# Sliding-window attention on one Trainium2 core: 16 heads to a step, the Exps issued right behind their logits, and a reordered start

## The chip, the cores and the metric

The kernel runs on one core of a Trainium2 chip. The metric is device time in microseconds (us below); the span that the profile gives, from the first to the last instruction, is about 2 us shorter. Executions of the kernel before lie between 1249 and 1257 us; each trace shows one execution.

Engine names as the profile has them: PE is TensorE (matmul), PEld its weight loads, DVE VectorE, ACT ScalarE, POOL GpSimd, SP SyncE, which here only issues DMAs. In this kernel matmuls write to PSUM and read their operands from SBUF, two on-chip memories; a DMA is a transfer that runs beside the engines.

## The reference, cut to what matters

```python
x = A_x                                        # 2048 x 576
x = x + A(layernorm(x)); x = x + B(layernorm(x))
x = x + A(layernorm(x)); x = x + B(layernorm(x))

def A(x):                                      # 32 heads of 18
    q, k, v = split(x @ wqkv)
    # each position attends to 8 positions: itself and 2, 4, ... 14 before it
    attn = softmax(q . k * scale over those 8)
    return (attn . v) @ wo

def B(x):                                      # gated MLP with a 2048 x 2048 mix over positions
    z1, z2 = split(gelu(x @ w_in))
    return (z1 * (w_sp @ layernorm(z2) + b_sp)) @ w_out
```

Below, layers 1 and 3 are the attention layers A, layers 2 and 4 the mixers B. The mixers take three quarters of the time and are not touched.

## The kernel before

A tile of 112 queries (19 tiles) takes a dense block of logits per head against 128 keys; a mask is built into the padded rows of Q and K, so that Exp alone makes the window. A head has 18 of 32 rows, so four heads lie in the four 32-row groups of the PE array. The loop works on a quarter tile `u` of 8 heads, and spreads other matmuls, the "fill work", over the loop from a table: the rest of the Q/K projections (`PG`), values (`VW`), output projections (`WO`).

```python
def H_tile(self, name):                    # logits: 2 buffers of 2 PSUM banks
    return self.ps.tile([P, 2, 512], f32, name=name, tag="H", bufs=2)
# O_tile: tag "O", 2 banks, probabilities x values.  PT_tile(any_bank=False): tag "PT", 2 banks, fill work

def L_mm(u):                               # logits of 8 heads: 2 row groups x 4 groups of heads
    t, hf, jp = half(u)
    L_tiles[u] = L_ps = self.H_tile("L_ps")
    for ftl in range(4):
        for jj in range(2):
            j = 2 * jp + jj                # row group 0,1 (jp 0) or 2,3 (jp 1)
            nc.tensor.matmul(L_ps[:nk, jj, ...], lhsT=kT[32*j:32*j+32, ...], rhs=qT[32*j:32*j+32, ...],
                             tile_position=(32 * j, 0), ...)
def EXP(u):                                # one ACTIVATE of 128 x 896, PSUM -> SBUF
    nc.scalar.activation(out=P_bufs[u % 4]..., in_=Lv..., func=ACT.Exp, scale=scale)
def PV(u): ...                             # 8 matmuls, 19 columns each, into O_ps
def NORM(u): ...                           # after every second u: DVE reciprocal and multiply into o_t;
                                           # after a whole tile SP transposes o_t into the ring oT by DMA
def PG(d, qk, cc, dve, queues): ...        # 5 matmuls, PSUM copy by DVE or ACT into stg, 7 stores into QK
def VW(t, hh, dve): ...                    # 5 matmuls, PSUM copy into v_ext
def WO(i, hh): ...                         # 5 matmuls on oT and wo_sb, add and layernorm on DVE and POOL

# ... cut: the start of layer 1 (loads, masks, layernorm, first projections) ...
for d, qk, cc in pgs[:4]:
    PG(d, qk, cc, False, q2)
for k_, (d, qk, cc) in enumerate(pgs[4:]):
    at((k_ * 30) // 16, PG, d, qk, cc, k_ % 2 == 0)
for i in range(NS):
    u = 4 * t + (12 if t < NT - 3 else 10) # t: the last tile that rows of block i need
    at(u, WO, i, 0); at(u + 1, WO, i, 1)   # ... and its loads, layernorm, stores
if li == 0:
    at(1, self.load_wo, nc.gpsimd)
L_mm(0)
for u in range(NU):                        # NU = 76
    EXP(u)
    if u + 1 < NU:
        L_mm(u + 1)
    for f, a in table.pop(u, []):          # fill work of this quarter
        f(*a)
    if u >= 1:
        PV(u - 1)
        if u % 2 == 0:
            NORM(u - 1)
```

In the traces here ACT works off its instructions in the order of the program (an example is at 656.21 us below). So Exp u+1 stands behind the PSUM copies of the fill work of quarter u, which wait for PE.

The softmax here doesn't subtract the row's maximum and nothing guards it: scores larger than these inputs give would overflow.

## Time and profile before

| | before |
|---|---|
| median | 1253.6 us (4 runs, 1250.1 to 1256.5) |
| span of the profiled execution (a fifth run, 1253.2 us) | 1250.7 us |
| start to the first logits of layer 1 | 52.7 us |
| loop of layer 1, first logits to last output projection | 118.2 us |
| layer 2 | 464.8 us |
| layer 3, projections ahead of the loop | 31.4 us |
| loop of layer 3 | 114.4 us |
| layer 4 | 469.2 us |

From the page, the share of the span that PE is busy, and the clock granted to it in 40 equal slices (9 is 90% or more):

```profile
PE 1204.0 (96%) x8428; PEld 647.5 (52%) x8528; DVE 542.2 (43%) x1202; ACT 388.4 (31%) x609; POOL 277.6 (22%) x371
...
PEclk9899999999999999999999999999999999999999
```

PE looks full. The same by stretches, one row each for the start, the loop of layer 1 (from its first in-loop projection at 57.0 us, behind the wait of 4.0 us below, to the mixer), layer 2, the loop of layer 3 (to the mixer) and layer 4. PEclk is the granted clock, as a share of full speed; the DMA share is the busy share of the 16 DMA engines as the profile reckons it, and can exceed 1:

```profile
core 0: us, PE busy (x) PEld busy (x) DVE busy (x) ACT busy (x) POOL busy (x), PEclk, DMA share, GB/s
0.00:52.70 52.70, 35.80 (x171) 17.91 (x176) 36.19 (x110) 22.18 (x35) 20.44 (x60) 0.97 0.62 155
57.00:163.70 106.70, 100.31 (x1564) 73.98 (x1572) 63.12 (x178) 70.71 (x98) 57.70 (x68) 0.98 0.74 159
171.00:635.70 464.70, 462.38 (x2438) 230.24 (x2474) 188.24 (x373) 106.14 (x179) 66.21 (x87) 1.00 0.25 64
667.00:775.60 108.60, 102.00 (x1602) 75.95 (x1609) 64.04 (x180) 75.14 (x104) 56.30 (x66) 1.00 0.80 169
781.50:1250.70 469.20, 462.80 (x2439) 229.93 (x2474) 168.98 (x310) 93.15 (x164) 55.48 (x57) 1.00 0.20 49
```

The mixers have no gaps worth naming: of the 6.4 us of layer 4 in which PE isn't busy the waits view names 1.3, and this trace lacks some matmul records (2439 in layer 4). In the loops PE is idle for 6 to 7 us each, at the start for 17. Whom PE waited for, longest in total first (us, times, longest):

```profile
PE L_ps L405 <- ACT P_sb L413: 11.6, 31, 0.8
...
PE pp L380 <- DMA xnT<-ln_xn: 4.0, 1, 4.0
...
PE pp L380 <- ACT stg L352: 2.9, 2, 2.0
```

The first line is the one that the change aims at: logits wait 31 times, in both layers together 11.6 us, for an Exp that frees their PSUM tile. The next two lines are the start. One more, left out here: output projections wait once, 1.3 us, for an `oT` transpose.

But a group that counts as busy can still be slow. From the timeline of PE in layer 3 (start us, length us, then the matmuls merged; what follows starts when the array lets it):

```profile
667.09 0.40 PE L405 MATMUL L_ps<-QK 32*128 32x112 bf16 x16
667.42 0.79 PE L358 MATMUL pv<-wv_sb,xnT 128*128 128x288 bf16 x5
...
672.07 0.35 PE L424 MATMUL O_ps<-v_ext,P_sb 128*128 128x19 bf16 x8
672.35 0.37 PE L405 MATMUL L_ps<-QK 32*128 32x112 bf16 x8
672.65 0.36 PE L424 MATMUL O_ps<-v_ext,P_sb 128*128 128x19 bf16 x8
673.72 0.37 PE L405 MATMUL L_ps<-QK 32*128 32x112 bf16 x8 [0.71 <-ACT P_sb L413]
```

Read it by starts, not by lengths: 8 logits matmuls hold PE from 672.35 to 672.65, 0.30 us. 16 in a row, which happens only where the loop begins, hold it from 667.09 to 667.42, 0.33 us. In the single records of the trace the 8 go in pairs 49 ns apart and leave a tail of 0.14 us; the 16 go in pairs about 25 ns apart. The last line is one of the waits.

### The profile page before, as it was taken

How to read it: one execution, taken by the hardware profiler on the slowest of the kernel's cores; microseconds unless marked ns; L12 is line 12 of the kernel's file. 1: busy time of each engine (PE TensorE's matmuls, PEld its weight loads, DVE VectorE, ACT ScalarE, POOL GpSimd, SP SyncE). 2: the span in 40 equal slices, each digit the busy share in tenths (PEclk: the TensorE clock that was granted, in tenths of full speed). 3: DMA queues.
4: the chain of work that ended last, by engine and by line, in shares of the span. 5: the costliest groups of instructions: out<-in, count | busy, mean ns of one | idle time of the engine just before them, and what ended most of it. 6: DMA issues, size and time to landing. Idle time of an engine off the chain costs nothing.

```text
span 1250.7 us, 20588 instructions
## 1 busy us (share of the span) xinstructions
PE 1204.0 (96%) x8428; PEld 647.5 (52%) x8528; DVE 542.2 (43%) x1202; ACT 388.4 (31%) x609; POOL 277.6 (22%) x371
## 2 busy tenths in 40 slices
PE   5799999999999999999998999999999999999998
PEld 3367754444444444447755677444444444444577
DVE  9246658633223323324552567674322332232321
ACT  4366757701110111011146676774011011101000
POOL 2346567400000000001132466772000000000000
PEclk9899999999999999999999999999999999999999
DMA  5678779000000000046644797960000000000342
GB/s 163 119 166 175 155 163 231 4 18 12 11 11 1 11 11 11 1 152 172 174 105 113 169 198 171 193 134 22 1 11 12 11 11 11 11 1 1 125 118 72
DMA packets 175686, 101.56 MB, mean 81 GB/s; under 512 B 134296, under 2 KB 155864, under 8 KB 175592
## 3 DMA queue, kind: packets, MB, share of 16 engines
q1 hardware_dynamic: 163632, 76.70, 27.6%
q0 software_dynamic: 6448, 17.67, 5.4%
q10 hardware_dynamic: 5512, 5.88, 1.5%
q8 instruction: 66, 1.08, 0.3%
q14 instruction: 28, 0.23, 0.1%
HBM read 42.39 MB, written 16.53 MB: 47 GB/s over the span
## 4 chain that ended last, share of the span: by engine, by line
PE 86%; POOL 3%; ACT 3%; issue 3%; DVE 2%; DMA 1%; SPq 1%; POOLq 0%; ACTq 0%; DVEq 0%
PE pg L794 40%; PE pz L776 12%; PE po L848 11%; PE pz L699 10%; PE pp L380 6%; PE pv L358 3%; ACT P_sb L413 2%; POOL ln_xn L235 2%; PE L_ps L405 2%; PE pw L453 2%; PE pzs L699 1%; PE O_ps L424 1%; DVE QK L182 1%; DVE ln_st L497 1%; ACT stg L352 1%
## 5 line engine op out<-in xcount | busy, mean ns | idle before, releaser
L794 PE MATMUL pg<-Wq,Z 128*128 128x512 bf16 x2256 | 500.0, 379 | 2.4
L794 PEld LDWEIGHTS <-Z 128*128 128x128 bf16 x2304 | 225.5, 98 | 271.8
L798 DVE TENSOR_TENSOR g_tmp<-pg,ln_xn 128x512 f32<-128x512 f32 x144 | 99.6, 692 | 429.1 <-PE pg L794 417.2
L788 ACT ACTIVATE z1T<-pz 128x1024 bf16<-128x1024 f32 x72 | 73.7, 1023 | 513.9 <-PE pz L776 513.7
L848 PE MATMUL po<-wout,Z 128*128 128x288 bf16 x1152 | 141.4, 286 | 0.0
L77 POOL DMA_DIRECT2D wout<-in_B_w_out_dram x4 | 4.3, 1064 | 604.6 <-PE pg L794 604.6
L776 PE MATMUL pz<-xnT,w 128*128 128x512 bf16 (+1 forms) x630 | 135.0, 380 | 1.1 <-issue 0.6
L413 ACT ACTIVATE P_sb<-L_ps 128x896 bf16<-128x896 f32 (+1 forms) x152 | 127.5, 893 | 12.1 <-PE L_ps L405 11.8
L848 PEld LDWEIGHTS <-Z 128*128 128x128 bf16 x1152 | 112.7, 98 | 28.8
L699 PEld LDWEIGHTS <-xnT 128*128 128x128 bf16 (+1 forms) x800 | 66.5, 97 | 82.6 <-issue 24.9
L380 PE MATMUL pp<-xnT,wqk_sb 128*128 128x512 bf16 x378 | 96.0, 394 | 10.4 <-DMA xnT<-ln_xn 4.0
L799 DVE TENSOR_TENSOR Z<-g_tmp,z1T 128x512 bf16<-128x512 f32 x144 | 99.7, 692 | 9.7
L699 PE MATMUL pz<-win2a,xnT 128*128 128x512 bf16 x366 | 101.2, 380 | 1.2 <-ACT zp L713 0.8
L776 PEld LDWEIGHTS <-w 128*128 128x128 bf16 (+1 forms) x640 | 51.1, 97 | 80.0 <-issue 27.1
L713 ACT ACTIVATE zp<-pz 128x1024 bf16<-128x1024 f32 x64 | 65.5, 1023 | 45.7 <-PE pz L699 30.2
L235 POOL TENSOR_SCALAR ln_xn<-x_new,ln_mv,ln_rstd 128x576 bf16<-128x576 f32 x32 | 75.5, 2361 | 3.3
L380 PEld LDWEIGHTS <-wqk_sb 128*128 128x128 bf16 x400 | 38.8, 101 | 54.2 <-issue 16.0
L858 DVE TENSOR_TENSOR x_new<-po,xo 128x288 f32<-128x288 f32 (+1 forms) x64 | 28.8, 456 | 87.8 <-PE po L848 87.8
L699 PE MATMUL pz<-win2b,xnT 128*128 128x512 bf16 (+1 forms) x256 | 65.9, 380 | 0.7
L405 PE MATMUL L_ps<-QK 32*128 32x112 bf16 (+1 forms) x1216 | 54.9, 208 | 11.9 <-ACT P_sb L413 11.6
L358 PE MATMUL pv<-wv_sb,xnT 128*128 128x288 bf16 (+1 forms) x380 | 60.6, 294 | 0.2 <-ACT xnT L516 0.2
L715 DVE CUSTOM_DVE_ANT_0 Z<-zp 128x1536 bf16<-128x1536 bf16 x32 | 56.2, 1756 | 7.8 <-ACT zp L713 7.8
(102 smaller groups left out, 932.0 us busy)
## 6 DMA issues: line engine op xcount, KB each, us to landing
xres<-x_new SPq DMA_DIRECT2D x48, 288.0 KB
xo<-xres SPq DMA_DIRECT2D x48, 288.0 KB
wout<-in_B_w_out_dram POOLq DMA_DIRECT2D x4, 1296.0 KB, 10.0
QK<-stg SPq DMA_DIRECT2D x64, 72.0 KB
QK<-stg POOLq DMA_DIRECT2D x64, 72.0 KB, 3.7
w<-in_B_w_in_dram SPq DMA_DIRECT2D x16, 256.0 KB
win2a<-in_B_w_in_dram POOLq DMA_DIRECT2D x12, 288.0 KB, 5.0
wqk_sb<-in_A_wqkv_dram ACTq DMA_DIRECT2D x2, 1152.0 KB
```

The costliest lines, as they stand in the source:

```text
L235: e.tensor_scalar(out=xn[:nrows, 0:D], in0=x_t[:nrows, :], scalar1=mv[:nrows, 0:1], scalar2=rstd[:nrows, 0:1], op0=ALU.subtract, op1=ALU.mult)
L358: nc.tensor.matmul(pv[:nk, 0:288], lhsT=self.xnT[:, c, QT * t:QT * t + nk], rhs=wv_sb[:, c, hh * 288:(hh + 1) * 288], start=(c == 0), stop ...
L380: nc.tensor.matmul(pp[:, :], lhsT=w, rhs=self.xnT[:, c, PADL + cc * 512:PADL + (cc + 1) * 512], start=(c == 0), stop=(c == 4))
L405: nc.tensor.matmul(L_ps[:nk, jj, ftl * QT:ftl * QT + nq], lhsT=kT[32 * j:32 * j + 32, g, QT * t:QT * t + nk], rhs=qT[32 * j:32 * j + 32, g ...
L413: nc.scalar.activation(out=P_bufs[u % 4][:nk, :, :, 0:nq], in_=Lv[:nk, :, :, 0:nq], func=ACT.Exp, scale=scale)
L699: nc.tensor.matmul(pzvs[ci][:, sub * 512:sub * 512 + w], lhsT=self.xnT[r0:r1, c, PADL + i * P:PADL + (i + 1) * P], rhs=win2(c)[r0:r1, c0 + ...
L776: nc.tensor.matmul(pz1s[q // 2][:, q % 2, :], lhsT=w1[r0:r1, c, sub * P:(sub + 1) * P], rhs=self.xnT[r0:r1, c, PADL + q * 512:PADL + (q + ...
L788: nc.scalar.activation(out=z1T[:, q2 * 512:(q2 + 2) * 512], in_=pz1s[q2 // 2][:, :, :].rearrange("p a b -> p (a b)"), func=ACT.Gelu_apprx_ ...
L794: nc.tensor.matmul(pg[:, :], lhsT=Z[:, jj, i, sub * P:(sub + 1) * P], rhs=Wq[q][:, i, :], start=(i == 0), stop=(i == NS - 1))
L798: nc.vector.tensor_tensor(out=tmp[:], in0=pg[:, :], in1=bsp[:, qs], op=ALU.add)
L799: nc.vector.tensor_tensor(out=uT(jj)[:, sub, qs], in0=tmp[:], in1=z1Ts[jj, sub][:, qs], op=ALU.mult)
L848: nc.tensor.matmul(acc[hh], lhsT=uT(j // 2)[:, j % 2, i * P:(i + 1) * P], rhs=wouts[j // NJH][:, j % NJH, hh * 288:(hh + 1) * 288], start= ...
```

## The change

The intent: a step now holds 16 heads of a tile (two logits tiles), its two Exps are issued at once behind the logits and ahead of the copies of the fill work, then come the values of the step before. All in-loop Q/K projections are copied by DVE, and the values' projections beside them by ACT. The start is reordered: masks are built first, their load moves from ACT's queue to SP's, 40 matmuls on the identity warm the PE clock, a layernorm is issued later. Two of three QK stores go to POOL's queue instead of one of two. The table of the fill work is counted in steps; the output projections move with it, from seven quarters (3.5 steps) behind the last values of their tile to three steps.

```diff
+            self.build_window_rows(sb)
+            self.load_pat(nc.sync)
+            self.make_ident()
+            warm = self.PT_tile([P, 512], f32, "warm", any_bank=False)
+            for _ in range(40):
+                nc.tensor.matmul(warm[:, 0:P], lhsT=self.ident[:], rhs=self.ident[:], start=True, stop=True)
             setup_bufs()
-            self.build_window_rows(sb)
-            self.load_pat(nc.scalar)
 ...
-            q2 = (nc.gpsimd, nc.sync)
+            q2 = (nc.gpsimd, nc.sync, nc.gpsimd)
 ...
-            at((k_ * PG_END) // len(pgs), PG, d, qk, cc, k_ % 2 == 0)      # PG_END 30, counted in u
+            at((k_ * PG_END) // len(pgs), PG, d, qk, cc, True)             # PG_END 14, counted in s
 ...
-            u = 4 * t + (12 if t < NT - 3 else 10)
+            s = 2 * t + (4 if t < NT - 3 else 3)
 ...
         L_mm(0)
-        for u in range(NU):
-            EXP(u)
-            if u + 1 < NU:
-                L_mm(u + 1)
-            for f, a in table.pop(u, []):
-                f(*a)
-            if u >= 1:
-                PV(u - 1)
-                if u % 2 == 0:
-                    NORM(u - 1)
+        EXP(0)
+        for s in range(NST):               # NST = 38; L_mm(s): 16 matmuls into 2 tiles, EXP(s): 2 ACTIVATEs
+            if s + 1 < NST:
+                L_mm(s + 1)
+                EXP(s + 1)
+            PV(s)                          # 16 matmuls, then the normalization
+            for f, a in table.pop(s, []):
+                f(*a)
```

## The prediction

> **What bounds it now.** The page shows PE busy 1204 of 1251 us. By stretches, the mixer layers (2 and 4) have almost no PE gaps and aren't touched. Open are the start, 0 to 57 us (PE busy 36), and the attention loops, 57 to 171 us (PE busy 106) and 668 to 782 us. In the waits view about 5.5 us per layer go to logits waiting for an Exp to free their PSUM tile: an Exp (0.87 us) queues on ACT behind fill copies (0.4 to 0.6 us), which wait for PE.
>
> "Busy" hides more. In the timeline 8 logits matmuls cost 0.30 us: pairs on two row groups 49 ns apart, then a 0.14 us tail. Twice (52.7 and 667 us) two groups run back to back, and all 16 take 0.33 us, pairs 25 ns apart: four row groups work at once. That fits the Trainium skill, "TensorE: Matmul & The Clock Gate", Part 3 (different row groups run concurrently). 8 probability-value matmuls cost 0.285 us, 16 cost 0.50.
>
> **The change, costed.** (1) A step holds 16 heads: logits and values fall from 1.17 to about 0.82 us, 0.35 x 37 steps = 13 us per layer, all on the PE path. (2) Exps go ahead of fill copies: 5 to 8 us of gaps mostly close. (3) New waits: one step now holds both logits tiles. ACT needs 2x0.87 + 0.2 to 0.4 = 2.0 to 2.2 us a step; PE about 3.3 us while projections fill (14 steps), but only 0.82+0.63+0.62 = 2.07 later, so they are level there: 4 to 5 us of new waits per layer, 1 to 2 at the loop's start, 1 at its end. Net: -15 us in layer 1, -11 in layer 3.
> (4) Start: ACT's first transposed copies stand behind the pattern load (11.0 to 14.2 us) that ACT issues; on SP's queue it frees them 3 us sooner. The 40 warm-up matmuls (about 4.3 us, before the input is normalized, so free) let the first value projections run at 0.63 instead of up to 1.2 us, 1.5 us more. (5) Two thirds of the QK stores go to POOL's queue; SP's queue (stores 0.85 us, transposes 1.3 to 1.7) gates PE at 54 to 57 us. Start in all: -5 us (3 to 8).
>
> **Sum:** -15 -11 -5 = -31 us; about 1 back for busier queues: 1222 us, 80% range 1206 to 1238. Faster by over 2% (below 1227.5): 0.70; within 2%: 0.28; slower: 0.02.
>
> **What would show it.** Logits 16 in about 0.33 us, pairs 25 ns apart, in most steps; values 16 in about 0.5; loops of 95 to 99 us instead of 114; logits' waits for Exp small in the projection part, short and frequent later; ACT over 85% busy later; first value projection at 13 us instead of 16.4; layer 1's in-loop fill beginning at 52 us instead of 57; mixers unchanged.
>
> **What would make it wrong.** If the second half of the logits usually waits for the second Exp, four row groups don't overlap and later steps lose most of (1), 12 us in all. If steps of 2.1 us (now 2.5) outrun the transposes: DMA busy share is already 0.77 in layer 1's later loop and 0.94 in layer 3's, and the output projection follows three steps after its transpose; PE would wait for oT. If DVE, which now copies all in-loop projections (0.69 us), blocks on a staging tile whose stores haven't landed, values wait. If ACT's hand-offs exceed 0.1 us, later steps take 2.3 us, 5 us more per layer.

## The result, and the profile after

The changed kernel takes 1235.7 us (median of 4 runs, 1234.6 to 1239.4) against 1253.6 of before. The ratio is 0.9864, with a 95% interval of 0.983 to 0.990: 1.4% faster. Ratios, here and below, are the mean time of a kernel's fast runs over that of the kernel before in the same rounds, so they are not quite the ratios of the medians quoted. The prediction said 1222, with 1206 to 1238 as its range: inside the range, but a little more than half of the gain forecast, and in the class "within 2%", to which it gave 0.28.

The same lines of the page, after:

```profile
PE 1198.0 (97%) x8568; PEld 624.5 (51%) x8568; DVE 545.6 (44%) x1206; ACT 385.5 (31%) x605; POOL 276.2 (22%) x380
...
PEclk9889999999999999999998999999999999999999
```

The clock row has two more slices below 9 than before: the third (61.6 to 92.5 us), which holds the first output projection of layer 1, and the 22nd (647 to 678 us), which holds the beginning of layer 3's loop. The stretches of the start, the loop of layer 1 (again from its first in-loop projection) and the loop of layer 3:

```profile
0.00:48.90 48.90, 38.33 (x212) 20.87 (x213) 35.24 (x110) 21.72 (x34) 23.25 (x64) 0.97 0.72 165
54.65:155.00 100.35, 93.15 (x1547) 60.53 (x1543) 66.12 (x181) 67.72 (x95) 58.48 (x69) 0.95 0.84 168
...
656.00:757.30 101.30, 95.23 (x1610) 63.07 (x1609) 66.33 (x182) 73.96 (x104) 57.08 (x67) 0.97 0.92 180
```

The mixers, left out here, are the same (465.2 and 468.8 us, PE idle for 3.4 us at most). The loops are 6 to 7 us shorter, but still have 6 to 7 us of idle PE each, and a mean clock of 0.95 and 0.97. The waits of PE:

```profile
PE L_ps L407 <- ACT P_sb L416: 6.1, 6, 2.6
...
PE pw L453 <- issue: 4.1, 1, 4.1
PE pp L383 <- ACT stg L355: 3.7, 2, 2.1
PE pw L453 <- DVE stg L353: 3.7, 14, 0.5
PE pw L453 <- DMA oT<-o_t: 2.5, 4, 1.3
```

The 31 short waits for Exps are down to 6, but half of their time is left, three of them at the loops' beginnings; and the waits of the output projection (`pw`) have grown: two of its lines are new, and the third, for the `oT` transposes, was 1.3 us before. One of the long waits is where the loop of layer 3 begins:

```profile
656.10 0.40 PE L407 MATMUL L_ps<-QK 32*128 32x112 bf16 x16
659.07 0.37 PE L407 MATMUL L_ps<-QK 32*128 32x112 bf16 x8 [2.58 <-ACT P_sb L416]
659.88 0.55 PE L407 MATMUL L_ps<-QK 32*128 32x112 bf16 x8 [0.44 <-ACT P_sb L416]
660.37 0.60 PE L427 MATMUL O_ps<-v_ext,P_sb 128*128 128x19 bf16 x16
660.81 4.43 PE L383 MATMUL pp<-xnT,wqk_sb 128*128 128x512 bf16 x10
665.03 1.40 PE L361 MATMUL pv<-wv_sb,xnT 128*128 128x288 bf16 x5
666.37 0.40 PE L407 MATMUL L_ps<-QK 32*128 32x112 bf16 x16
666.69 0.56 PE L427 MATMUL O_ps<-v_ext,P_sb 128*128 128x19 bf16 x16
667.11 1.24 PE L383 MATMUL pp<-xnT,wqk_sb 128*128 128x512 bf16 x5
```

With both logits tiles held by step 0, the logits of step 1 can't start before the first Exps end. ACT in that time:

```profile
656.21 0.59 ACT L355 CAST stg<-pp 128x512 bf16<-128x512 f32 x1 [0.45 <-PE pp L383]
656.81 1.28 ACT L416 ACT_TABLE_LOAD   x1
658.11 3.35 ACT L416 ACTIVATE P_sb<-L_ps 128x896 bf16<-128x896 f32 x4
```

Ahead of the first Exp stand a copy and the load of the function table, 1.28 us. Before, the same load was mostly covered by fill work behind the second logits (a wait of 0.8 us was left). Then the ten projection matmuls at 660.81 take until 665.03, 0.42 us each, where the five at 667.11 take 0.22 us each. That is the clock: the granted clock is 0.50 from 659.5 to 666.2 us. The Trainium skill, "TensorE: Matmul & The Clock Gate", Part 1 and "Why this matters for your kernels", says that PE runs at half rate after at least one idle window of about 3.4 us, needs a busy one to return, and that these windows run freely. This trace agrees in the half rate and in the length, which is two such windows, 6.8 us. It agrees less in the idle time that it takes: here 3.0 us, broken by 8 logits, were enough, and over all runs idle time alone does not tell. Half rate followed 2.0 us in e4 (below), and none followed 3.3 us in e8. A gap of 2.1 us ahead of layer 3's loop is the same in 12 of the 14 traces, and half rate followed it in six of them.

The second new gap is in layer 1, at its first output projection:

```profile
72.48 0.78 PE L361 MATMUL pv<-wv_sb,xnT 128*128 128x288 bf16 x5
77.40 1.36 PE L453 MATMUL pw<-wo_sb,oT 128*128 128x288 bf16 x5 [4.14 <-issue]
...
79.65 3.77 PE L383 MATMUL pp<-xnT,wqk_sb 128*128 128x512 bf16 x10
```

4.1 us of idle PE, put down to nothing by the waits view (what it was is settled under e4 to e6), and a slow clock behind it. The granted clock in 10 us from each gap (layer 1 loop start, this one, layer 3 loop start):

```profile
48.90:58.90 10.00, 6.43 (x60) 2.73 (x60) 1.41 (x3) 4.54 (x6) 0.00 (x0) 0.66 0.51 71
73.40:83.30 9.90, 5.90 (x48) 2.75 (x49) 1.86 (x4) 2.02 (x3) 2.93 (x5) 0.66 1.10 166
656.10:666.40 10.30, 7.29 (x68) 3.33 (x69) 2.10 (x4) 5.21 (x6) 0.00 (x0) 0.67 0.00 0
```

What the change was for, works. A pair of late steps in layer 1:

```profile
140.73 0.55 PE L407 MATMUL L_ps<-QK 32*128 32x112 bf16 x16
141.22 0.56 PE L427 MATMUL O_ps<-v_ext,P_sb 128*128 128x19 bf16 x16
...
142.95 0.40 PE L407 MATMUL L_ps<-QK 32*128 32x112 bf16 x16
143.28 0.56 PE L427 MATMUL O_ps<-v_ext,P_sb 128*128 128x19 bf16 x16
```

16 logits take 0.33 us (142.95 to 143.28) or 0.49 (140.73 to 141.22, where the second half waits for an Exp), 16 values 0.42. Together 0.75 us where the four groups of before took 1.17: 0.27 us of the saving is in the logits, 0.15 in the values. Over both layers 43 batches of logits take 0.33 or 0.34 us, and 20, all in the later parts, 0.48 to 0.50.

Where the 17.9 us of the profiled executions come from, by sections (us, ends read from the trace; "b1" is the best kernel of the experiments below):

| section | before | after | b1 |
|---|---|---|---|
| start to first logits, layer 1 | 52.7 | 48.9 | 47.1 |
| layer 1, first logits to last in-loop projection | 53.0 | 55.8 | 48.5 |
| layer 1, from there to the first mixer matmul | 58.0 | 50.3 | 49.9 |
| layer 1, tail to the last output projection | 7.2 | 5.7 | 6.3 |
| layer 2 | 464.8 | 465.5 | 466.1 |
| layer 3, ahead of the loop | 31.4 | 29.9 | 27.8 |
| layer 3, first logits to last in-loop projection | 50.7 | 50.7 | 43.5 |
| layer 3, from there to the first mixer matmul | 57.8 | 50.4 | 49.7 |
| layer 3, tail | 5.9 | 6.6 | 6.7 |
| layer 4 | 469.2 | 469.0 | 469.5 |

The later parts of both loops gave about 7.5 us each. The projection parts gave nothing in layer 3 and lost 2.8 us in layer 1. That is the part that holds the new gaps.

Two entries need care. "Layer 3, ahead of the loop" is 1.5 us shorter after, but the program there differs only in the queues of the QK stores, and the traces show another reason: the gap of 2.1 us named above was followed by half rate in the trace of before (0.50 from 641.0 to 644.3 us) and not in the trace of after. Other runs of the changed start show both lengths. So these 1.5 of the 17.9 us can't be put down to the change. And in b1 two projections, 2.2 us of this section, have moved behind the first logits.

### The profile page after: what moved, and what is told of

Its sections match the earlier page's. It is cut to its first block, busy times and chain, and to the rows that moved or that the text cites. A ratio compares the mean times of both kernels' runs of the same rounds, so it can differ in the third digit from the quotient of the medians.

```text
span 1232.8 us, 20796 instructions
## 1 busy us (share of the span) xinstructions
PE 1198.0 (97%) x8568; PEld 624.5 (51%) x8568; DVE 545.6 (44%) x1206; ACT 385.5 (31%) x605; POOL 276.2 (22%) x380
## 4 chain that ended last, share of the span: by engine, by line
PE 88%; DMA 1%; DVE 1%; ACT 1%; issue 0%; POOL 0%; DVEq 0%; POOLq 0%; ACTq 0%
PE pg L795 40%; PE pz L777 12%; PE po L849 11%; PE pz L700 10%; PE pp L383 3%; PE pw L453 3%; PE pv L361 2%; PE O_ps L427 2%; PE L_ps L407 2%; PE pzs L700 1%; DMA oT<-o_t 1%; DVE stg L353 0%; ACT P_sb L416 0%; DVE ln_st L214 0%; ACT stg L355 0%
## 5 line engine op out<-in xcount | busy, mean ns | idle before, releaser
L383 PE MATMUL pp<-xnT,wqk_sb 128*128 128x512 bf16 x400 | 99.4, 400 | 6.4 <-ACT stg L355 3.7
L700 PE MATMUL pz<-win2a,xnT 128*128 128x512 bf16 x384 | 104.5, 380 | 0.0
L77 POOL DMA_DIRECT2D QK<-stg x74 | 48.1, 653 | 65.1 <-issue 26.9
L453 PE MATMUL pw<-wo_sb,oT 128*128 128x288 bf16 x320 | 49.6, 288 | 10.5 <-issue 4.1
```

The costliest lines, as they stand in the source:

```text
L383: nc.tensor.matmul(pp[:, :], lhsT=w, rhs=self.xnT[:, c, PADL + cc * 512:PADL + (cc + 1) * 512], start=(c == 0), stop=(c == 4))
L453: nc.tensor.matmul(pw[:, 0:288], lhsT=oT[:, c, r0:r0 + P], rhs=wo_sb[:, c, hh * 288:(hh + 1) * 288], start=(c == 0), stop=(c == 4))
L700: nc.tensor.matmul(pzvs[ci][:, sub * 512:sub * 512 + w], lhsT=self.xnT[r0:r1, c, PADL + i * P:PADL + (i + 1) * P], rhs=win2(c)[r0:r1, c0 + ...
```

## The experiments

Twelve kernels ran, all with correct results. The theory: batching 16 heads saves PE time as forecast, and the missing half of the gain sits in three new waits (first Exps, first output projection, the output projection's PSUM bank) and the slow clock that follows two of them. The rivals are named with each run.

### e1 and e2: the start alone, the loop alone

e1 is the kernel before with the hunks of the start and the QK stores; e2 is the kernel before with the hunks of the loop.

> The kernel before with only the reordered start, the warm-up matmuls and the new split of the QK stores; the loops stay as they were. If the parts add up: the first value projection at 12.7 us as in the changed kernel, the first in-loop projection of layer 1 at about 53 to 55 us instead of 57, so 2 to 4 us faster than before (1250 us, ratio 0.997 to 0.998). Rival: the start is worth the 5 us that the prediction gave it and the loop hides it in the changed kernel: 1247 to 1248 us, ratio 0.995 to 0.996.

> The kernel before with only the 16-head loop. If the parts add up: 14 us faster than before (ratio 0.989), with the bubble at the start of both loops (4 to 5 us of idle PE, then projections at about 0.43 us per matmul instead of 0.22) and the 4 us wait of the first output projection of layer 1 present as in the changed kernel. Rival: these waits come from the new start and the QK store split; then they are absent and the kernel is 20 us or more faster than before (ratio 0.984 or less).

Measured: e1 1248.4 us, ratio 0.9984 (0.996 to 1.001), 2 us, an interval that includes no gain. e2 1240.5 us, ratio 0.9919 (0.989 to 0.995).

In e1's trace the first Q/K projection starts 6.2 us earlier (15.6 us instead of 21.8), the first logits 2.6 us, the last in-loop projection 1.9 us, the mixer 0.7 us. So the start does what it says, and most of it is lost again on the way: between the first projection and the first logits PE now waits longer for ACT's copies into the staging tiles (5.3 us against 2.9 before), and ACT for stores of these tiles that have not landed (7.1 us against 6.1). The later part of the old loop is 1.2 us longer: in this trace the granted clock is 0.50 from 128.2 to 131.6 us, which costs about that much; no gap is ahead of it that would explain it. The execution traced is also the slowest of e1's four (1252.1 us; the others 1248.1 to 1248.5). The rival, 5 us, fell.

e2 shows the bubbles with the old start too: at the start of both loops the wait and the slow projections (ten take 3.7 us in layer 1 and 3.2 in layer 3, against 2.2 at the full clock). The wait of the first output projection is there too (2.7 us at 80.0 us, and here the profile names the `oT` transpose as what ended it), so both come with the loop and the rival fell. And e2 pays elsewhere: its tail of layer 1 is 9.9 us instead of 5.7, with a wait of 2.0 us for an `oT` transpose and half rate behind it (0.50 from 158.2 to 164.9 us). The parts, 2 and 10 us, do not add up to 17. The 4 us of that tail are most of the difference.

### e3: batching undone, the place of the Exps kept

```diff
-            if s + 1 < NST:
-                L_mm(s + 1)            # 16 heads
-                EXP(s + 1)
-            PV(s)
+            for jp in range(2):        # 8 heads
+                if s + 1 < NST:
+                    L_mm(s + 1, jp)
+                    EXP(s + 1, jp)
+                PV(s, jp)
```

> The changed kernel with the logits and values of a step issued by 8 heads again (8 logits, Exp, 8 values, twice), Exps still ahead of the fill copies. Theory A, row groups working together and fewer switches between kinds of matmul carry the gain: logits plus values cost 1.17 us a step again instead of 0.75, 0.42 us x 37 steps x 2 layers = up to 31 us slower than the changed kernel, about 1260 us (ratio 1.00 to 1.01). Rival B, moving the Exps ahead of the copies carries it: within 5 us of the changed kernel (ratio 0.986 to 0.990).

Measured: 1245.1 us, ratio 0.9965 (0.993 to 1.000), 10 us slower than the changed kernel: between the two theories. The trace has the 1.1 us per step of A. But its slower steps reach the first output projection when the transpose has nearly landed (1.2 us of wait instead of 4.1), and the waits for `oT` fell from 2.5 to 0.9 us. That could hide part of the cost; b3 below repeats the test without these waits. Set beside e1, which has the same start (ratio 0.9984), e3 also says what the rest of the new loop, the Exps ahead of the copies above all, is worth without the batch: about 2 us, not resolved.

### e4, e5, e6: the first output projection of layer 1

Three ways to take away what it may wait for: load its weights at the start (e4), run every output projection two steps later (e5), or push the loads of the next layer's weights back (e6).

```diff
 e4     self.load_wqk(nc.scalar)
+e4     self.load_wo(nc.scalar)
-e4     at(1, self.load_wo, nc.gpsimd)
-e5     s = 2 * t + (4 if t < NT - 3 else 3)
+e5     s = 2 * t + (6 if t < NT - 3 else 3)
-e6     at(2 + 2 * k_, f)              # f: a piece of win2a
+e6     at(8 + k_, f)
```

> The changed kernel with the load of the output projection's weights of layer 1 issued at the start, from ACT's queue, instead of in the loop. Theory A, the first output projection of layer 1 (4.1 us of idle PE at 73 to 77 us, then a cold clock for 5 us) waits for the transpose of oT behind the loads and stores: nothing changes there, ratio 0.985 to 0.987. Rival B, it waits for its weights: the wait goes, and 4 to 6 us with the clock, ratio 0.981 to 0.983.

> The changed kernel with each output projection two steps later behind its tile (6 instead of 4), weights loaded in the loop as before. e4 showed that the first wait goes when the weights' load is moved away; it left open whether the weights themselves or the transposes behind their traffic were late. Under both, four more microseconds of slack remove the wait at 73 to 77 us and the slow clock after it: last in-loop projection of layer 1 at 98 to 100 us instead of 104.9, the waits for oT in the later steps gone too, 5 to 7 us in all, ratio 0.981 to 0.983. Rival, the time is given back later in the loop, because something paced by the DMA engines sets its end: 0 to 2 us, ratio 0.985 to 0.987.

> The changed kernel with the six loads of the next layer's weights (win2a) issued from step 8 on instead of step 2, the output projection's weights still loaded in the loop ahead of them on the same queue. Theory T, the first output projection waits for the transposes of oT, which share the DMA engines with these loads: the wait of 4.1 us falls to under 2. Theory W, it waits for its own weights, which are ahead of these loads: it stays at 3.5 us or more. The total may move either way by 3 us, because the loads then meet the later transposes.

| | median us | ratio (95%) | wait of the first output projection | layer 1, to last projection / from there to mixer |
|---|---|---|---|---|
| after | 1235.7 | 0.9864 (0.983 to 0.990) | 4.1 | 55.8 / 50.3 |
| e4 | 1231.8 | 0.9844 (0.982 to 0.987) | 0.2 | 49.1 / 53.6 |
| e5 | 1225.3 | 0.9784 (0.976 to 0.981) | 0.2 | 47.3 / 51.3 |
| e6 | 1232.5 | 0.9843 (0.982 to 0.987) | 2.3 | 53.2 / 49.8 |

e4 removed the wait, so theory A in the words it was given ("nothing changes there") fell. It did not make its rival true. In the changed kernel the weights were issued at 62.7 and 63.4 us and had landed by 70.2 us; the wait ended at 77.4 us. The first output projection needs the transposes of the first two tiles. They were issued at 62.3 and 68.9 us, the second behind four QK stores in SP's queue:

```profile
65.30 3.47 SPq L77 DMA_DIRECT2D QK<-stg  x4
68.90 1.23 SPq L438 DMA_TRANSPOSE oT<-o_t  x1
```

In the trace's records of semaphores (the counters by which a DMA reports that it has landed) the last report of the first transpose comes at 69.9 us and that of the second at 77.3, just before PE goes on. So the second transpose is what is late: it took 8.4 us from issue to landing. It took 7.0 us in e6, which leaves the weights where they are and takes other traffic away, and 4.4 us in e4. In e2 and e8 the waits view itself names the transpose. So the traffic around it, the weights among it, is why; the DMA share was 1.20 from 68.9 to 77.3 us. The wait of 2.3 us is not the "under 2" that e6 was to show, and the share of each load is not settled. In the kernel before the same transpose took 7.2 us, and nothing waited, since 12.3 us lay between its issue and the projection; in the changed kernel it would have been 4.4 without the wait. The Trainium skill, "Trainium Kernel Development and Optimization", section "Key Constraints", says that DMAs of all queues run on the same 16 engines and interleave; e4 and e6, which only move loads on other queues, agree: 3.9 and 1.9 us less wait for a transpose on SP's queue.

e4 gained little in the end: what it won up to the last projection, 6.7 us, it lost by 1.4 us at the start and 3.3 us in the later part, where a transpose was late again (2.0 us, 119.5 to 121.5, and half rate behind it until 124.7 us). e5 gives all output projections two steps more, so five behind their tile where before had 3.5 and the change three, and 11.8 us from the issue of the second transpose to its use. It keeps the gain: 10 us, more than the 5 to 7 expected. About 2.7 us of it are in layer 3, where two output projections, each with the bank wait of e8 below, leave the projection part for the later part (47.1 and 51.3 us for the two parts, against 50.7 and 50.4).

### e7: work behind the first Exps

```diff
-        for d, qk, cc in pgs[:4]:
+        for d, qk, cc in pgs[:2]:
             PG(d, qk, cc, False, q2)
+        L_mm(0)
+        EXP(0)
+        for d, qk, cc in pgs[2:4]:
+            PG(d, qk, cc, False, q2)
```

> The changed kernel with two of the four projections ahead of the loop issued behind the first logits and Exps, so that PE has work while ACT loads its table (1.28 us) and computes the first two Exps. Layer 3: the gap of 3.0 us and the slow clock behind it (ten projections in 4.2 us instead of 2.2) mostly go, 3 to 5 us. Layer 1: its second logits also wait for the QK stores of the last heads until 54 us, so 0 to 1 us there. In all 3 to 5 us, ratio 0.982 to 0.984. Rival, the gap moves to the second logits: under 1 us.

Measured: 1233.8 us, ratio 0.9846 (0.982 to 0.988); against the changed kernel's 0.9864 that is not resolved. The trace resolves it: in layer 3 the gap of 3.0 us became two of 0.3 and 0.4 us, the projections behind it run at 0.22 us, and the section from the first projection to the mixer fell from 131.1 to 127.3 us. In layer 1, whose second logits wait for QK stores until 54 us, nothing was won, as expected; and the later part there was 4 us longer, with 5.7 us of waits for `oT` in all against 2.5, one of them of 3.2 us with half rate behind it. Again a late transpose ate a gain.

### e8: the output projection's PSUM bank

```diff
-            pw = self.PT_tile([P, 512], f32, "pw", any_bank=False)
+            pw = self.O_tile([P, 512], f32, "pw")
```

A step of the projection part needs three fill tiles, and the fill work has two banks: the third, `pw`, waits until DVE has copied the first.

> The changed kernel with the output projection's tile in the PSUM banks of the values instead of those of the fill work. The waits of the output projection for DVE's copy of the projection (14 waits, 3.7 us in both layers) go: 3 to 4 us, ratio 0.983 to 0.985. Rival, they turn into waits of the values for DVE: no gain.

Measured: 1228.9 us, ratio 0.9808 (0.978 to 0.983): 7 us, twice what was expected. The waits are gone and did not turn into waits of the values for DVE. In layer 3 seven steps of the projection part hold an output projection; they fell from about 3.6 to 3.15 us each, 3.1 us together, and the six such steps of layer 1 behind its first by 2.8 us. That is 6 of the 7 us. The waits view had charged these steps 0.17 to 0.47 us each, so each wait cost about 0.16 us more than its idle time; why, no run shows. (The whole projection part of layer 3 is 4.5 us shorter in this trace; the other 1.4 are at the loop's start, where half rate lasted for 3.4 us instead of 6.8, which the edit did not aim at.) The first output projection of layer 1 waits here too; the waits view names the transpose, and no half rate follows (ten projections in 2.15 us):

```profile
77.89 0.77 PE L453 MATMUL pw<-wo_sb,oT 128*128 128x288 bf16 x5 [3.30 <-DMA oT<-o_t]
...
79.35 2.32 PE L383 MATMUL pp<-xnT,wqk_sb 128*128 128x512 bf16 x10
```

### e9: the Exps behind the fill work, batches of 16 kept

```diff
             if s + 1 < NST:
                 L_mm(s + 1)
-                EXP(s + 1)
             PV(s)
             for f, a in table.pop(s, []):
                 f(*a)
+            if s + 1 < NST:
+                EXP(s + 1)
```

> The changed kernel with the two Exps of a step issued on ACT after the fill work of the same step instead of ahead of it; batches of 16 stay. If batching alone carried the change and the place of the Exps were a side matter: within 10 us of the changed kernel. If batching needs it, because a step holds both logits tiles: where a step has a fill copy on ACT, the next logits wait until that copy and then both Exps are done, so such steps grow by 1 to 1.8 us; over some 50 steps in the two layers 50 to 90 us slower, 1285 to 1325 us.

Measured: 1300.1 us, ratio 1.038 (1.035 to 1.041). The waits of logits for Exps:

```profile
PE L_ps L407 <- ACT P_sb L416: 54.9, 91, 2.6
```

So the two halves of the change are not two gains. Batching takes away the second logits tile that let the old loop run ahead; only with the Exps issued at once is the batch worth having.

### b1, b2, b3: the repairs together, and batching measured again

b1 is the changed kernel with e4, e5, e7 and e8 together. b2 adds, for layer 1, that the QK stores of the last four heads of the first half all go through POOL's queue. b3 is b1 with the batching undone as in e3.

> All four repairs on the changed kernel: output projections two steps later, their weights of layer 1 loaded at the start, two projections behind the first Exps, the output projection's tile in the values' PSUM banks. If the causes are the ones named and independent: 10 us (e5), 3 to 4 for the bank, 3 to 4 for the first Exps of layer 3, together 16 to 18 us below the changed kernel, 1217 to 1220 us, ratio 0.972 to 0.975. Rival, the loops are by then held by ACT or the DMA engines and the gains overlap: 1222 to 1226 us, ratio 0.976 to 0.979.

> As b1, and the QK stores of the last four heads of layer 1's first half all go through POOL's queue, where they don't stand behind the four transposes of SP's queue: the second logits of layer 1, which waited for a QK store until 54 us, start by 51 us and the first in-loop projection, then held by the transposes of xnT only, by 53 us: 1 to 2 us below b1. Rival, the transposes hold it as long: no difference to b1.

> b1 with the logits and values of a step issued by 8 heads again, as e3 did to the changed kernel. e3 cost 10 us where 31 were expected; part of that may be that its slower steps also avoided the wait of the first output projection and some waits for oT, which b1 doesn't have. Then the whole cost of small batches shows here: 0.37 us x 14 steps x 2 in the projection part and about 0.2 us x 24 x 2 in the later part (where the batched step waits for ACT), 18 to 22 us, so 1234 to 1239 us. Rival, batching really is worth only 10 us: 1224 to 1228 us.

| | median us | ratio (95%) |
|---|---|---|
| b1 | 1216.5 | 0.9712 (0.969 to 0.973) |
| b2 | 1216.7 | 0.9712 (0.969 to 0.973) |
| b3 | 1235.5 | 0.9865 (0.985 to 0.988) |

b1 beats both kernels: 36 us under before, 19 under the changed kernel. The gains of the repairs add up (10 of e5, 7 of e8, 2 of e7; e4 aims at a wait that e5 already removes), and `pw` is no longer among the longest waits of its PE. b2 won 1.7 us in layer 1 up to the mixer and lost 1.4 us in the projections ahead of layer 3's loop, which were 29.2 us instead of 27.8; no difference, as its rival said. Both shifts go with the clock: b1's trace has half rate from 41.5 to 45.0 us, ahead of its first logits, and b2's from 621.8 to 625.2. b3, which lacks b2's edit, has the same early first logits as b2 (45.2 us against b1's 47.1). So b2's edit shows no effect of its own.

b3 settles e3: without the waits that e3 happened to avoid, small batches cost 19 us (18 to 22 expected). A late step of b3, and the beginning of the next:

```profile
125.37 0.37 PE L409 MATMUL L_ps<-QK 32*128 32x112 bf16 x8
125.67 0.36 PE L433 MATMUL O_ps<-v_ext,P_sb 128*128 128x19 bf16 x8
125.97 0.37 PE L409 MATMUL L_ps<-QK 32*128 32x112 bf16 x8
126.27 0.36 PE L433 MATMUL O_ps<-v_ext,P_sb 128*128 128x19 bf16 x8
126.48 0.77 PE L361 MATMUL pv<-wv_sb,xnT 128*128 128x288 bf16 x5
...
127.80 0.37 PE L409 MATMUL L_ps<-QK 32*128 32x112 bf16 x8
```

A step takes 2.43 us (125.37 to 127.80), 1.11 of it logits and values. In the later part (24 steps) b3 needs 55.8 us and b1 49.9 in layer 1, so 0.25 us per step instead of the 0.36 that PE saves, because there the batched step is held by ACT. What small batches cost has two parts that no run takes apart: the row groups of the logits working together, and fewer changes between kinds of matmul. The traces show both, 0.33 us for 16 logits against 0.49 where one half follows the other, and 0.15 us less for 16 values.

## Why the prediction was right or wrong

**The mechanism was right.** Logits 16 take 0.33 us in most steps, as forecast from two places of the trace before; values 16 take 0.42 instead of the 0.50 used. b3 minus b1 gives 19 us for batching in both layers. The prediction's 13 us per layer less 4 to 5 of new waits in the later part, so 17 in all, is close. ACT is the limit there, as forecast: 41.6 us busy in the 50 us from 105 to 155 us, 83% where "over 85%" was said, and a step takes 2.10 us (50.3 over 24) where 2.07 to 2.2 was said.

**The size was off by the third term**, "new waits". The prediction had 1 to 2 us at the loop's start. It measured more, and two waits were not in the sum at all:

| term, as the prediction put it | forecast | measured |
|---|---|---|
| "1 to 2 at the loop's start" | 1 to 2 a layer | layer 3: 3.0 of gap and 2.7 of slow clock; layer 1: 2.1 of slow clock, of which before had 1.5 |
| first output projection ("PE would wait for oT", named among what could go wrong, not in the sum) | 0 | 4.1 of gap and 2.3 of slow clock in layer 1 |
| fill work's third tile against two banks | 0 | 0.45 a step: 3.1 in the seven steps of layer 3 and 2.8 in six of layer 1, 6 in all, by e8 against the changed kernel |
| values of 16 in 0.50 | 0 | 0.42, so up to 6 better (0.08 x 76 steps), and 2 if only the 28 steps of the projection parts count, since ACT holds the later ones |
| start | -5 (3 to 8) | -3.8 at the first logits, -2.4 at the first in-loop projection; -2 for e1 alone |

The slow-clock figures are differences: ten projections took 4.25 us at 54.65 and 4.22 at 660.81, against 2.16 for ten at the full clock, and so on for the other matmuls behind each gap. With these terms: -31 + 4 (layer 3) + 1 (layer 1) + 6 (first output projection) + 6 (bank) - 6 (values) + 2 (start) = -18 us, or -14 with 2 for the values; measured -17.9, of which 1.5 are the clock ahead of layer 3's loop. The sum is as good as its estimates, no better, and that one form of it meets the measured number is partly luck.

Point by point:

- "5 to 8 us of gaps mostly close": they did, 31 waits of 11.6 us became 6 of 6.1 us, but three of the six, 5.0 us, are the new ones at the loops' starts. The 5.5 us won are used up by the waits of `pw`: the loops are as idle as before.
- "a step holds both logits tiles": right, and e9 shows how much hangs on it (64 us). What was overlooked at the loop's start was the table load of 1.28 us and the copy in front of the first Exp, and that the slow clock behind the gap of 3.0 us costs nearly as much again (2.7).
- "steps outrun the transposes": happened, in layer 1 at 73 us. The prediction gave it no time and looked for it in the later steps; the place where it failed is in the projection part, where QK stores, weights and transposes meet on the DMA engines and a transpose took 8.4 us to land.
- "If DVE blocks on a staging tile": hardly (one wait of 0.4 us for a store in the projection parts). DVE mattered in another way, by the delay of its copy against two banks.
- Start: "first value projection at 13 us" was right (12.7), and so was the warm-up: 30 value matmuls take 3.8 us (12.66 to 16.45) instead of 5.4. "Fill at 52 us" was wrong (54.65): between the two stand QK stores and staging tiles, which the earlier start only meets sooner.
- "mixers unchanged": right within 0.7 us.

**Still open:** how the lateness of single transposes falls. e4 and e7 lost 3 to 4 us in their later parts, where waits for `oT` stood at different places, and no run tells which traffic it was. Nor does any run tell what share of idle time lowers the clock: half rate came behind some gaps of 2 us and not behind one of 3.3. With e5's extra slack few waits for `oT` are left (one of 1.9 us in e5, one of 0.8 in b1).

## What to carry to other kernels

Batching small matmuls paid here (19 us by b3), but a batch that takes all buffers of a stage needs its consumer issued at once, and work for PE at the point where the pipeline is first filled. When a loop is sped up, go through what was scheduled a fixed number of steps behind (transposes, weights, PSUM banks): its slack shrinks with the step, and here the rewritten loop had shortened the distance itself as well. Two more steps of distance were worth more than half as much as the whole change (10 of 17.9 us). A gap on PE of 2 to 4 us may have to be counted nearly twice, because of the clock after it, and whether it has can differ between two traces of the same stretch of program; before a difference of 1 to 2 us in one section is explained, look at the granted clock there.

## What the Trainium skill lacked or had wrong

- "TensorE: Matmul & The Clock Gate", Part 3, "The mechanism", says that matmuls start and end strictly in program order. In this trace they don't, between row groups: of 16 logits issued as 8 on row groups 0 and 1 and then 8 on 2 and 3, the one that carries the second half's own wait starts 27 ns after the first of all (666.392 after 666.365 us), while the last of the first half (the one that raises its semaphore) starts at 666.526 and that of the second at 666.553. The two halves run interleaved, which is why 16 cost 0.33 us and 8 cost 0.30. It is not the program's order that is interleaved: in the batch at 140.73 us, whose second half had to wait for an Exp, all eight of the first half start ahead of it (until 140.895, the second half from 140.911).
- No page gives a time for going from 32-row matmuls back to full ones ("TensorE: Matmul & The Clock Gate" would be the place). Here the next group starts 0.14 us after the last logits matmul, whether 8 or 16 went before; that tail is nearly half of the 0.30 us of a group of 8.
- "ScalarE: Activation LUTs", "What ACT_TABLE_LOAD costs", gives about 1.28 us for the load and 1.38 more for a drain. The load agrees (1.28 us at 656.81); no drain shows here: the copy before it ended at 656.80 and the first Exp began at 658.11.
- "TensorE: Matmul & The Clock Gate", Part 1, gives at least one idle window of about 3.4 us as what lowers the clock. Here an idle of 2.0 us was enough (e4, half rate from 121.4 us), and in e1 half rate came at 128.2 us behind 8.1 us in which PE was busy for 7.3 and waited for 0.5 us at a time at most; that 3.3 us of idle in e8 had no half rate behind them fits. The Part also describes short idles that lower the clock, but what share of busy time keeps it is not on the page, and no run here measures it.
- "Trainium Kernel Development and Optimization", "Performance Expectations", says that matmul busy time is a bad measure of how near a kernel is to its limit, and that MFU and the busy share of LDWEIGHTS are good ones. These runs agree in the first: in the stretch 107 to 147 us e3 has PE busy for 40.0 of 40 us and the changed kernel for 39.3, and e3 is the slower of the two by 10 us. The busy time of the weight loads does not tell the two apart either: 29.3 us in e3 and 29.4 in the changed kernel.
